# A chunk's plain pair second, rows set aside in SBUF, and another order at the end of the first pass, in a fused FFT and feed-forward kernel

## The chip, the core and the metric

One core of a Trainium2 chip runs the kernel. The metric is the time of one execution on the device, in microseconds (us); several executions are timed and the median is given.

## The reference

The input `x` is 4 batches of 3008 rows of 256 numbers. The first stage is a Fourier filter, the second a feed-forward network over all 12,032 rows:

```python
X = np.fft.rfft(x, axis=1)
Yr = Xr @ w_r - Xi @ w_i + b_r          # 256 x 256 weights
Yi = Xr @ w_i + Xi @ w_r + b_i
Y  = soft_threshold(Yr, 0.01) + 1j * soft_threshold(Yi, 0.01)
y  = np.fft.irfft(Y, n=3008, axis=1)    # becomes 12032 rows of 256
h  = y @ w_in                            # 256 -> 2048
g  = np.maximum(h, 0) + alpha * np.minimum(h, 0)
out = g @ w_out                          # 2048 -> 256
```

## The kernel before

Every float32 operand of a large product is held as a high and a low part, and a product is three matmuls (high x high, low weight x high, high x low). PSUM is eight banks: four of pool `ps_f`, two of `ps_h`, two of `ps_o`.

**The Fourier stage** is a chain of small matmul groups a, b, m, c (L375 to L578) for each batch, all of which take banks of `ps_f`. Its last link turns 376 rows at a time (a group `dg`) back to the row domain: `s_dmm` (L612) makes two banks `ps_d`, and `s_dpart` (L616) splits them into the high and low tiles (`yh`, `yl`) of a chunk of 512 rows; ACT writes the high part (L629) and DVE subtracts for the low part (L631). Since 376 does not divide 512, many groups have rows for two chunks. The tiles of a chunk are opened by `y_open`; there are two sets, so the third chunk in a row must wait for the last use of the first.

**The feed-forward network, first form.** Nine chunks (`CC`) are worked on while the Fourier stage of batches 1 to 3 runs between their steps. A step (`l1_step`, L664) makes one of the 16 tiles of 128 hidden columns: six matmuls into `ps_h` (L659), ACT makes q (L669), DVE q (L670), ACT the high part (L672), and DVE or POOL the low part (L674). `l2_step` does the products of the step two before with `w_out` (L683 to L685 in `products`). Chunks 0 and 1 are interleaved (the first pass), because the second half of the weights is still being made from the raw weights (`conv_second`: L283, L277 to L280, L286, L287), pumped a piece at a time from inside the steps; `PAT` says how many pieces each step pumps. When a chunk is through, `turn` (L697) transposes its two accumulators on DVE (L701) into `oT`, of which there is one buffer, and `put` issues the stores of `oT` on the SP queue (L329) behind everything queued there.

**The second form.** The last 15 chunks (numbers n = 0 to 14; the last has 256 rows) go in pairs t = 0 to 7 of hidden tiles, by a Strassen-like scheme: `s_l1` (L745) makes two tiles (L659; ACT L751, DVE L752), `s_sums` (L756) makes seven operands (ACT L767, L778, L779; DVE L773, L775, L776, L777, L780; POOL L781), and `s_l2` (L828) does seven half-width products into four accumulators p and q (`ps_o`) and u and v (`ps_f`). One pair of each chunk, that in `PLAIN`, is done without the scheme: `z_parts` (L784) makes the high parts on ACT (L788) and the two low parts on POOL and DVE (L789), and `s_l2` does four full-width products into p and q. In the kernel before, `PLAIN` is pair 0. At the end of a chunk `s_out` (L849) folds the four accumulators: two copies on ACT (L855, L856) and six operations on DVE (L857 to L862).

The order is written out by hand. In step k of the second form the program emits: the first-layer tiles of pair k, the products of pair k - 2, at a chunk's end `s_out`, then `s_sums` of pair k. Every engine works through its instructions in this order. So at step (n + 1, t = 1) DVE has L752 twice, then `s_out` of chunk n, then the sums of pair 1; only then comes L752 of pair 2, which frees the `ps_h` bank that the first-layer matmuls of pair 3 write.

Of the kernel before, what the change touches and what calls it, by code (L numbers as in the profile page):

```python
# [9 lines left out]
F32 = mybir.dt.float32  # L10
# [5 lines left out]
AF = mybir.ActivationFunctionType  # L16
# [80 lines left out]
def fft_mix_moe(ctx, tc, x, w_r, w_i, b_r, b_i, w_in, w_out, alpha, la, rb, lc, rd, lf, cf, sel, out):  # L97
# [3 lines left out]
    CT = C // 128  # L101
    FT = DFF // 128
    R = 32
    CH = 4
# [13 lines left out]
    work = ctx.enter_context(tc.tile_pool(name="work", bufs=2))  # L118
    dram = ctx.enter_context(tc.tile_pool(name="dram", bufs=4, space=bass.MemoryType.DRAM))
    ps_f = ctx.enter_context(tc.tile_pool(name="ps_f", bufs=4, space=bass.MemoryType.PSUM))  # L120
    ps_h = ctx.enter_context(tc.tile_pool(name="ps_h", bufs=2, space=bass.MemoryType.PSUM))
    ps_o = ctx.enter_context(tc.tile_pool(name="ps_o", bufs=2, space=bass.MemoryType.PSUM))

    V, G, A, PE = nc.vector, nc.gpsimd, nc.scalar, nc.tensor

    def f(t):
        return t.bitcast(F32)
# [27 lines left out]
    FH = FT // 2  # L155
# [424 lines left out]
    zt, yt = {}, {}  # L580
# [8 lines left out]
    def d_mm(t, ct):  # L589
        ps = ps_f.tile([128, CH, 128], F32, tag="f", name="ps_d")  # L590
        for i in range(CH):
            PE.matmul(ps[:, i, 0:NP], t[:, i, 128 * ct:128 * ct + 128], rd_s, start=True, stop=True)  # L592
        return ps
# [9 lines left out]
    def d_parts(dg):  # L603

        s, e = TOK * dg, TOK * dg + TOK
        for c in range(s // SC, (e - 1) // SC + 1):
            a, z = max(s, SC * c), min(e, SC * (c + 1))
            yield c, (a - s) // CH, (z - s) // CH, a - SC * c, z - SC * c

    ds = {}  # L610

    def s_dmm(dg):  # L612
        t = zt.pop((dg // NCH, dg % NCH))
        ds[dg] = [d_mm(t, ct) for ct in range(CT)]

    def s_dpart(dg, c):  # L616
        parts = []
        for k, n0, n1, a, z in d_parts(dg):
            if k == c:
                for ct in range(CT):  # L620
                    ps = ds[dg][ct][:, :, n0:n1]
                    ys = [y[ct] for y in yt[c]]
                    if c == LASTC:
                        hi, lo = (y[:, a:z].rearrange("p (n i) -> p n i", i=CH) for y in ys)
                        parts.append((ps.rearrange("p i n -> p n i"), hi, lo))
                    else:
                        parts.extend(s_dput(ps, ys, a // CH, z // CH))
        for src, hi, lo in parts:
            A.activation(out=hi, in_=src, func=AF.Copy)  # L629
        for src, hi, lo in parts:  # L630
            V.tensor_tensor(out=lo, in0=src, in1=f(hi), op=ALU.subtract)  # L631

    def s_dput(ps, ys, u, u1):

        ys = [y.rearrange("p (g i j) -> p g i j", i=CH, j=32) for y in ys]
        n = 0
        while u < u1:
            if u % 32 == 0 and u1 - u >= 32:
                w = (u1 - u) // 32 * 32
                src = ps[:, :, n:n + w].rearrange("p i (g j) -> p g i j", j=32)  # L640
                dst = [y[:, u // 32:(u + w) // 32] for y in ys]
            else:
                w = min(u1, u // 32 * 32 + 32) - u
                src = ps[:, :, n:n + w]
                dst = [y[:, u // 32, :, u % 32:u % 32 + w] for y in ys]
            yield src, *dst
            u += w
            n += w
# [28 lines left out]
    def block(m, h):  # L677
        w = wo_h[m // FH][:, m % FH].rearrange("p w (c h) -> p w h c", h=2)
        return w[:, 0, h], w[:, 1, h]

    def products(prods):
        for (wh, wl), (gh, gl), o, first, last in prods:
            PE.matmul(o, wh, gh, start=first, stop=False)  # L683
            PE.matmul(o, wl, gh, start=False, stop=False)  # L684
            PE.matmul(o, wh, gl, start=False, stop=last)  # L685
# [18 lines left out]
    HS = SC // 2  # L704
    PR = FT // 2
# [37 lines left out]
    sg, sa, sq = {}, {}, {}  # L743
# [12 lines left out]
    def s_sums(n, t):  # L756
        q = sq.pop((n, t))
        if n == NS2 - 1 or t in PLAIN:
            z_parts(n, t, q)
# [24 lines left out]
    def z_parts(n, t, q):  # L784
        g = []
        for j, tags in enumerate((("xh", "Yh"), ("xl", "Yl"))):
            hi, lo = (work.tile([128, SC], F32R, tag=tag, name="zg")[:, 0:q.shape[2]] for tag in tags)
            A.activation(out=hi, in_=q[:, j], func=AF.Copy)  # L788
            (V if j else G).tensor_tensor(out=lo, in0=q[:, j], in1=f(hi), op=ALU.subtract)  # L789
            g.append((hi, lo))  # L790
        sg[n, t] = g
# [35 lines left out]

    def s_l2(n, t):  # L828
        if t == 0:
            sa[n] = [ps_o.tile([128, 2, HS], F32, tag="o", name="ps_o") for _ in range(2)]  # L830
        if t == 1:
            sa[n] += [ps_f.tile([128, 2, HS], F32, tag="f", name="ps_o") for _ in range(2)]
        if t in PLAIN:
            for j, g in enumerate(sg.pop((n, t))):
                products([(block(2 * t + j, h), g, sa[n][h].rearrange("p k n -> p (k n)"), (t, j) == (0, 0), False)
                     for h in range(2)])
            return
        r, z = t == 1, t == PR - 1
        b11, b22, b21, t1, t3, t2, t4 = sg.pop((n, t))
        s1, s2, s3, s4 = ([x[:, t] for x in sw[k]] for k in range(4))  # L840
        p, q, u, v = sa[n]
        products([(block(2 * t, 0), b11, u[:, 0], r, False), (block(2 * t + 1, 0), b21, p[:, 1], False, False),
             (s4, b22, p[:, 0], False, z), (s3, t3, v[:, 0], r, False),
             (s1, t1, v[:, 1], False, z), (s2, t2, u[:, 1], False, z),
             (block(2 * t + 1, 1), t4, q[:, 1], False, z)])

    so = {}

# [36 lines left out]
    J = 2  # L885
# [5 lines left out]
    MP = [2.5, 3.5, 3.5, 3.5, 3.5, 4, 4, 4.5]  # L891
    MM, M2, CM = 1.5, 3, 6
    SLAG = 2
    PLAIN = (0,)
    PAT = [0, 0] + [1, 1, 2] * 10
    NG = R // 2
    EARLY = 4
# [14 lines left out]
    with tc.manual_schedule():  # L912
# [98 lines left out]
        for dg in range(2):  # L1011
            s_dmm(dg)
            s_dpart(dg, 0)
# [4 lines left out]
        put()  # L1018

        steps = [(c, m) for c in range(J) for m in range(FH)]  # L1020
        steps += [(c, m + j) for m in range(FH, FT, 2) for c in range(J) for j in range(2)]
        steps += [(c, m) for c in range(J, CC) for m in range(FT)]
        NS = len(steps)
        todo = {}
# [1 line left out]
        def at(i, fn, *args, when=todo):  # L1026
            when.setdefault(i, []).append((fn, args))

        at(0.5, y_open, 1)
        at(0.5, s_dpart, 1, 1)  # L1030
        at(4.5, s_dmm, 2)
        at(4.5, s_dpart, 2, 1)
        at(5.5, y_open, 2)
        at(5.5, s_dpart, 2, 2)
        at(29, load_lc)
# [6 lines left out]
        for dg in range(3, B * NCH):  # L1042
            cs = [c for c, *_ in d_parts(dg)]
            i = FT * (cs[-1] - 1)
            if cs[-1] > CC:
                break
            if len(cs) == 2:
                i -= 2.5
                at(i, s_dmm, dg)
                at(i, s_dpart, dg, cs[0])  # L1050
                at(FT * (cs[-1] - 1) - 1, s_dpart, dg, cs[1])
            else:
                i += 8
                at(i, s_dmm, dg)
                at(i, s_dpart, dg, cs[0])
            at(i - 4, d_load, dg // NCH, dg % NCH)
        for b in range(B - 1):
            if b == 0:
                for g in range(FILL, NG):
                    i = 4 * (g - FILL) + 8  # L1060
# [4 lines left out]
            else:  # L1065
                for g in range(NG):
                    i = AO[b + 1] + (5 * g // 2) / 2
# [5 lines left out]
            for q in range(NPAIR):  # L1073
                i = BO[b + 1] + BP * q
# [15 lines left out]
        i = NS - 17  # L1090
# [10 lines left out]
        for dg in range(dg, B * NCH):  # L1101
            cs = [c for c, *_ in d_parts(dg)]
# [36 lines left out]
        for k in range(len(spairs) + SLAG):  # L1139
            do(pre, k)  # L1140
            if k < len(spairs):
                s_l1(*spairs[k])
            do(post, k)
            put()
            if k < SLAG:
                l2(NS - 1 + k)
            if k >= SLAG:
                n, t = spairs[k - SLAG]
                if n == NS2 - 1:
                    z_l2(t)  # L1150
                else:
                    s_l2(n, t)
                    if t == PR - 1:
                        s_out(n)
            if k < len(spairs):
                s_sums(*spairs[k])
            if k >= SLAG and t == 1 and n:
                s_turn(n - 1)
# [33 lines left out]
```

## Time and profile before

| | |
|---|---|
| median of 3 runs | 1401.27 us (1400.9 to 1404.81) |
| profiled execution, its own time | 1404.03 us |
| its span, first to last instruction | 1402.3 us |
| PE (TensorE matmuls) busy | 1351.0 us, 96% of the span |
| DVE, ACT, POOL busy | 1042.4, 729.2, 376.3 us |
| mean granted TensorE clock | 0.988 of full speed |

A busy share is a mean over stages with different limits. The first form with the Fourier stage runs from about 102 to 704 us of the span, the second form from there to the end. A granted clock of 1.00 is 2.4 GHz and one of 0.50 is 1.2 GHz.

### The profile page before, as it was taken

How to read it: one execution, taken by the hardware profiler on the slowest of the kernel's cores; microseconds unless marked ns; L12 is line 12 of the kernel's file. 1: busy time of each engine (PE TensorE's matmuls, PEld its weight loads, DVE VectorE, ACT ScalarE, POOL GpSimd, SP SyncE). 2: the span in 40 equal slices, each digit the busy share in tenths (PEclk: the TensorE clock that was granted, in tenths of full speed). 3: DMA queues.
4: the chain of work that ended last, by engine and by line, in shares of the span. 5: the costliest groups of instructions: out<-in, count | busy, mean ns of one | idle time of the engine just before them, and what ended most of it. 6: DMA issues, size and time to landing. Idle time of an engine off the chain costs nothing.

```text
span 1402.3 us, 22147 instructions
## 1 busy us (share of the span) xinstructions
PE 1351.0 (96%) x7866; PEld 1173.4 (84%) x7866; DVE 1042.4 (74%) x1843; ACT 729.2 (52%) x1423; POOL 376.3 (27%) x366
## 2 busy tenths in 40 slices
PE   9999998899999999999999999999999999999998
PEld 5978777788888888888888988898888889888988
DVE  2767866667777767677777787788778877877786
ACT  3556544545455544444555555565555555555554
POOL 3843552212222222222222221221212222222222
PEclk9999999999999999999999999999999999999999
DMA  8973333332243312120110110011011001101000
GB/s 224 250 219 97 104 102 101 103 107 84 65 131 94 104 62 87 38 83 24 27 38 12 27 38 7 21 28 27 12 27 28 15 24 27 27 12 28 16 16 24
DMA packets 103759, 89.74 MB, mean 64 GB/s; under 512 B 62446, under 2 KB 85849, under 8 KB 103648
## 3 DMA queue, kind: packets, MB, share of 16 engines
q1 hardware_dynamic: 95744, 77.68, 19.7%
q0 software_dynamic: 4912, 7.76, 2.0%
q10 hardware_dynamic: 2992, 2.88, 0.6%
q8 instruction: 62, 1.02, 0.3%
q14 instruction: 49, 0.40, 0.1%
HBM read 50.76 MB, written 34.34 MB: 61 GB/s over the span
## 4 chain that ended last, share of the span: by engine, by line
PE 66%; DVE 9%; ACT 2%; issue 2%; DMA 0%; POOL 0%; DVEq 0%; SPq 0%; ACTq 0%
PE ps_h L659 29%; PE ps_o L683 8%; PE ps_o L684 8%; PE ps_o L685 8%; PE ps_m L493 4%; PE ps_d L592 3%; PE ps_b L430 2%; DVE sq L752 1%; DVE dl L776 1%; DVE q L670 1%; DVE c L859 1%; DVE t L773 1%; DVE c L862 1%; ACT sq L751 1%; DVE Yt L537 1%
## 5 line engine op out<-in xcount | busy, mean ns | idle before, releaser
L659 PE MATMUL ps_h<-yh,w 128*128 128x512 f32 (+1 forms) x1472 | 502.3, 396 | 26.3 <-DVE sq L752 26.3
L659 PEld LDWEIGHTS ps_h<-yh,w 128*128 128x128 f32 x1472 | 280.3, 192 | 87.8 <-DVE sq L752 32.7
L659 PE MATMUL ps_h<-yl,w 128*128 128x512 f32 (+1 forms) x736 | 289.7, 394 | 0.0
L781 POOL TENSOR_TENSOR l<-t,h 128x512 fp32r<-128x512 f32 x98 | 126.8, 1294 | 503.7 <-ACT h L779 483.6
L752 DVE SCALAR_TENSOR_TENSOR sq<-sq,beta_s,ps_h 128x512 f32<-128x512 f32 (+1 forms) x240 | 168.1, 725 | 72.6 <-ACT sq L751 72.1
L672 ACT ACTIVATE gh<-q 128x512 fp32r<-128x512 f32 x144 | 90.9, 632 | 160.4 <-DVE q L670 160.3
L674 POOL TENSOR_TENSOR gl<-q,gh 128x512 fp32r<-128x512 f32 x69 | 91.7, 1329 | 281.0 <-ACT gh L672 266.5
L670 DVE SCALAR_TENSOR_TENSOR q<-q,beta_s,ps_h 128x512 f32<-128x512 f32 x144 | 106.9, 743 | 73.7 <-ACT q L669 72.9
L659 PEld LDWEIGHTS ps_h<-yl,w 128*128 128x128 f32 x736 | 141.0, 192 | 22.9 <-DVE yl L631 0.2
L751 ACT ACTIVATE sq<-ps_h 128x512 f32<-128x512 f32 (+1 forms) x240 | 132.7, 578 | 46.7 <-PE ps_h L659 44.8
L767 ACT ACTIVATE dh<-sq 128x768 fp32r<-128x768 f32 x98 | 83.0, 847 | 79.9 <-DVE sq L752 63.2
L683 PE MATMUL ps_o<-gh,w 128*128 128x512 f32 x288 | 116.4, 404 | 2.1 <-DVE oT L701 2.1
L779 ACT ACTIVATE h<-t 128x512 fp32r<-128x512 f32 x98 | 62.0, 633 | 104.8 <-DVE t L777 81.5
L685 PE MATMUL ps_o<-gl,w 128*128 128x512 f32 x288 | 114.4, 397 | 0.9 <-POOL gl L674 0.8
L684 PE MATMUL ps_o<-gh,w 128*128 128x512 f32 x288 | 114.3, 397 | 0.0
L669 ACT ACTIVATE q<-ps_h 128x512 f32<-128x512 f32 x144 | 85.2, 592 | 55.1 <-PE ps_h L659 53.0
L776 DVE TENSOR_TENSOR dl<-sq,dh 128x768 fp32r<-128x768 f32 x98 | 93.3, 952 | 0.0
L674 DVE TENSOR_TENSOR gl<-q,gh 128x512 fp32r<-128x512 f32 x75 | 59.3, 791 | 45.1 <-ACT gh L672 45.1
L778 ACT ACTIVATE h<-t 128x512 fp32r<-128x512 f32 x98 | 61.8, 630 | 44.7 <-DVE t L773 44.1
L685 PE MATMUL ps_o<-l,sw_a 128*128 128x256 f32 x294 | 82.0, 279 | 0.0
L683 PE MATMUL ps_o<-h,sw_a 128*128 128x256 f32 x294 | 81.9, 279 | 0.0
L773 DVE TENSOR_TENSOR t<-sq 128x512 f32<-128x512 f32 x98 | 67.5, 689 | 2.4
(184 smaller groups left out, 3002.4 us busy)
## 6 DMA issues: line engine op xcount, KB each, us to landing
zt<-zd SPq DMA_DIRECT2D x32, 384.0 KB
zd<-zst SPq DMA_DIRECT2D x37, 256.0 KB
ad<-ast SPq DMA_DIRECT2D x48, 192.0 KB
bt<-ad SPq DMA_DIRECT2D x72, 128.0 KB
out<-oT SPq DMA_DIRECT2D x248, 32.0 KB
xt<-in_x SPq DMA_DIRECT2D x21, 320.0 KB
cw_s<-in_moe_w_in SPq DMA_DIRECT2D x8, 512.0 KB
cw_s<-in_moe_w_out SPq DMA_DIRECT2D x8, 512.0 KB
```

The lines of the kernel that those rows point to most:

```text
L659: PE.matmul(ps, wi_h[m // FH][:, w, ct, 128 * (m % FH):128 * (m % FH) + 128], a[ct][:, 0:n], start=(k == 0), stop=(k == 3 * CT - 1))
L669: A.activation(out=q, in_=ps, func=AF.Relu, scale=-1.0)
L670: V.scalar_tensor_tensor(out=q, in0=q, scalar=beta_s[:, m:m + 1], in1=ps, op0=ALU.mult, op1=ALU.add)
L672: A.activation(out=hi, in_=q, func=AF.Copy)
L674: (V if by_v else G).tensor_tensor(out=lo, in0=q, in1=f(hi), op=ALU.subtract)
L683: PE.matmul(o, wh, gh, start=first, stop=False)
L684: PE.matmul(o, wl, gh, start=False, stop=False)
L685: PE.matmul(o, wh, gl, start=False, stop=last)
L751: A.activation(out=q[:, j], in_=ps, func=AF.Relu, scale=-1.0)
L752: V.scalar_tensor_tensor(out=q[:, j], in0=q[:, j], scalar=beta_s[:, m:m + 1], in1=ps, op0=ALU.mult, op1=ALU.add)
L776: V.tensor_tensor(out=dl, in0=q[:, HS:], in1=f(dh), op=ALU.subtract)
L781: G.tensor_tensor(out=l24, in0=t24, in1=f(h24), op=ALU.subtract)
```

## The change

Three edits, and one thing that goes with them.

1. `PLAIN` becomes pair 1. Pair 0 of a chunk now goes through the scheme and is the one that starts the four accumulators, so all four are opened at t = 0. In the plain pair, now second, the first matmul into q is cut into two of 256 columns, because one half of q holds sums by then and the other does not.
2. `s_daside` copies the rows of a group that belong to the later chunk from PSUM to a tile in SBUF (tag `zt`), on ACT, two copies for a group; `s_dpart` of the later chunk then reads that tile. It is called for groups 2, 4, 5, 6, 8, 9, 10 and 12, in the first form alone, right behind the earlier chunk's `s_dpart`.
3. The first pass ended with tiles 8 to 15 in turns, two of chunk 0 and two of chunk 1. Now tiles 8 to 11 go so, and then come tiles 12 to 15 of chunk 0 and tiles 12 to 15 of chunk 1. So in steps 26 and 27 stand tiles 14 and 15 of chunk 0, which were in steps 28 and 29; tiles 12 and 13 of chunk 1 go the other way.

```diff
+    def s_daside(dg, c):
+        n0, n1 = next((n0, n1) for k, n0, n1, *_ in d_parts(dg) if k == c)
+        t = work.tile([128, CT, CH, 86], F32, tag="zt", name="hd")
+        for ct, ps in enumerate(ds[dg]):
+            A.activation(out=t[:, ct, :, 0:n1 - n0], in_=ps[:, :, n0:n1], func=AF.Copy)
+        ds[dg] = [t[:, ct] for ct in range(CT)]
+        moved[dg] = n0
...
     def s_l2(n, t):
         if t == 0:
-            sa[n] = [ps_o.tile([128, 2, HS], F32, tag="o", name="ps_o") for _ in range(2)]
-        if t == 1:
-            sa[n] += [ps_f.tile([128, 2, HS], F32, tag="f", name="ps_o") for _ in range(2)]
+            sa[n] = [ps_o.tile([128, 2, HS], F32, tag="o", name="ps_o") for _ in range(2)] \
+                + [ps_f.tile([128, 2, HS], F32, tag="f", name="ps_o") for _ in range(2)]
...
+                        if (j, h) == (0, 1) and w is wh and g is gh:
+                            for k in range(2):
+                                PE.matmul(o[:, HS * k:HS * k + HS], w, g[:, HS * k:HS * k + HS], start=False, stop=False)
+                        else:
+                            PE.matmul(o, w, g, start=False, stop=False)
...
-        r, z = t == 1, t == PR - 1
+        r, z = t == 0, t == PR - 1
...
-    PLAIN = (0,)
+    PLAIN = (1,)
...
-        steps += [(c, m + j) for m in range(FH, FT, 2) for c in range(J) for j in range(2)]
+        steps += [(c, m + j) for m in range(FH, FT - 4, 2) for c in range(J) for j in range(2)]
+        steps += [(c, m) for c in range(J) for m in range(FT - 4, FT)]
...
+        at(4.5, s_daside, 2, 2)
...
                 at(i, s_dpart, dg, cs[0])
+                at(i, s_daside, dg, cs[1])
                 at(FT * (cs[-1] - 1) - 1, s_dpart, dg, cs[1])
```

## Rows read from the trace of the kernel before

**Rows 1.** The page: busy time, share of the span and instructions of each engine.

```profile
PE 1351.0 (96%) x7866; PEld 1173.4 (84%) x7866; DVE 1042.4 (74%) x1843; ACT 729.2 (52%) x1423; POOL 376.3 (27%) x366
```

**Rows 2.** Waits of PE, whole run: us in total, times, longest us.

```profile
PE ps_h L659 <- DVE sq L752: 26.3, 15, 1.9
PE ps_m L493 <- DVE Xl L455: 5.7, 1, 5.7
```

**Rows 3.** Chain that ended last, in order of time: start, us, what.

```profile
765.17 3.02 PE ps_h L659 x12
...
861.28 4.61 PE ps_h L659 x12
868.37 2.75 PE ps_h L659 x12
...
1341.94 3.01 PE ps_h L659 x12
```

**Rows 4.** Windows: us, PE busy, granted clock (PEclk), DMA share, GB/s.

```profile
863.00:864.00 1.00, 1.00 (x3) 0.50 0.00 0
```

**Rows 5.** Timeline of one chunk's end: start, us, engine, instruction [idle before <-releaser].

```profile
903.03 0.39 ACT L855 ACTIVATE se<-ps_o 128x256 f32<-128x256 f32 x1 [1.51 <-PE ps_o L685]
...
903.44 0.42 DVE L857 TENSOR_TENSOR su<-ps_o,se 128x256 f32<-128x256 f32 x1 [1.15 <-ACT se L855]
...
905.94 0.39 PE L683 MATMUL ps_o<-zg,w 128*128 128x512 f32 x1
...
906.02 0.69 DVE L862 TENSOR_TENSOR c<-ps_o,se 128x512 f32<-128x512 f32 x1
...
906.63 0.68 DVE L773 TENSOR_TENSOR t<-sq 128x512 f32<-128x512 f32 x1
...
906.76 0.19 PEld L683 LDWEIGHTS ps_o<-zg,w 128*128 128x128 f32 x1 [0.40 <-DVE c L862]
...
908.89 0.69 DVE L780 TENSOR_TENSOR l<-t,h 128x512 fp32r<-128x512 f32 x1
...
910.24 1.41 DVE L752 SCALAR_TENSOR_TENSOR sq<-sq,beta_s,ps_h 128x512 f32<-128x512 f32 x2 [0.66 <-ACT sq L751]
...
911.04 0.50 PE L659 MATMUL ps_h<-yh,w 128*128 128x512 f32 x1 [1.91 <-DVE sq L752]
```

**Rows 6.** Groups by line, 700 to 1340 us: busy, mean ns of one, idle before.

```profile
L789 DVE TENSOR_TENSOR zg<-sq,zg 128x512 fp32r<-128x512 f32 x14 | 15.7, 1123 | 17.9 <-ACT zg L788 17.9
...
L789 POOL TENSOR_TENSOR zg<-sq,zg 128x512 fp32r<-128x512 f32 x14 | 18.1, 1296 | 21.5 <-PE ps_o L684 15.2 <-ACT zg L788 6.3
```

**Rows 7.** Timeline of DVE, the two steps behind that end.

```profile
915.28 1.40 DVE L752 SCALAR_TENSOR_TENSOR sq<-sq,beta_s,ps_h 128x512 f32<-128x512 f32 x2 [0.64 <-ACT sq L751]
...
920.81 1.37 DVE L752 SCALAR_TENSOR_TENSOR sq<-sq,beta_s,ps_h 128x512 f32<-128x512 f32 x2
```

**Rows 8.** Timeline of DVE and of SP's queue, chunks 0 and 1 turned.

```profile
199.86 1.31 DVE L701 STREAM_TRANSPOSE oT<-ps_o 128x512 f32<-128x512 f32 x2
...
212.28 1.31 DVE L701 STREAM_TRANSPOSE oT<-ps_o 128x512 f32<-128x512 f32 x2 [6.18 <-DMA bt<-ad]
...
201.20 9.78 SPq L329 DMA_DIRECT2D out<-oT  x20
```

**Rows 9.** Timeline of PE (step 26) and POOL, end of the first pass.

```profile
178.91 0.39 PE L659 MATMUL ps_h<-xh,w 128*128 128x512 f32 x1
...
179.91 1.34 POOL L287 TENSOR_TENSOR w<-conv 128x512 fp32r<-128x512 f32 x1 [1.58 <-DVE conv L286]
...
186.60 1.30 POOL L287 TENSOR_TENSOR w<-conv 128x512 fp32r<-128x512 f32 x1
```

**Rows 10.** Timeline of PE, three stops at banks of `ps_f`.

```profile
271.92 0.71 PE L385 MATMUL ps_a<-xh,la_s 94*96 94x512 f32 x1 [2.11 <-DVE Yc L531]
...
280.47 0.48 PE L385 MATMUL ps_a<-xh,la_s 94*96 94x512 f32 x1 [1.97 <-ACT zst L572]
...
589.01 0.71 PE L493 MATMUL ps_m<-wr_s,Xh 128*128 128x256 f32 x4 [1.31 <-DVE Yc L531]
```

More of the change, by code (lines that the diff above doesn't have):

```diff
@@ L614, in s_dmm @@
         ds[dg] = [d_mm(t, ct) for ct in range(CT)]
+    def s_daside(dg, c):
[5 more added lines that the diff above has]
+        moved[dg] = n0
+    moved = {}
     def s_dpart(dg, c):
@@ L619, in s_dpart @@
             if k == c:
+                n0, n1 = n0 - moved.get(dg, 0), n1 - moved.get(dg, 0)
                 for ct in range(CT):
@@ L829, in s_l2 @@
         if t == 0:
-            sa[n] = [ps_o.tile([128, 2, HS], F32, tag="o", name="ps_o") for _ in range(2)]
-        if t == 1:
-            sa[n] += [ps_f.tile([128, 2, HS], F32, tag="f", name="ps_o") for _ in range(2)]
+            sa[n] = [ps_o.tile([128, 2, HS], F32, tag="o", name="ps_o") for _ in range(2)] \
+                + [ps_f.tile([128, 2, HS], F32, tag="f", name="ps_o") for _ in range(2)]
         if t in PLAIN:
-            for j, g in enumerate(sg.pop((n, t))):
-                products([(block(2 * t + j, h), g, sa[n][h].rearrange("p k n -> p (k n)"), (t, j) == (0, 0), False)
-                     for h in range(2)])
+            for j, (gh, gl) in enumerate(sg.pop((n, t))):
+                for h in range(2):
+                    (wh, wl), o = block(2 * t + j, h), sa[n][h].rearrange("p k n -> p (k n)")
+                    for w, g in ((wh, gh), (wl, gh), (wh, gl)):
+                        if (j, h) == (0, 1) and w is wh and g is gh:
[3 more added lines that the diff above has]
+                            PE.matmul(o, w, g, start=False, stop=False)
             return
-        r, z = t == 1, t == PR - 1
+        r, z = t == 0, t == PR - 1
         b11, b22, b21, t1, t3, t2, t4 = sg.pop((n, t))
@@ L841, in s_l2 @@
         p, q, u, v = sa[n]
-        products([(block(2 * t, 0), b11, u[:, 0], r, False), (block(2 * t + 1, 0), b21, p[:, 1], False, False),
+        products([(block(2 * t, 0), b11, u[:, 0], r, False), (block(2 * t + 1, 0), b21, p[:, 1], r, False),
              (s4, b22, p[:, 0], False, z), (s3, t3, v[:, 0], r, False),
              (s1, t1, v[:, 1], False, z), (s2, t2, u[:, 1], False, z),
-             (block(2 * t + 1, 1), t4, q[:, 1], False, z)])
+             (block(2 * t + 1, 1), t4, q[:, 1], r, z)])
     so = {}
```

## The prediction

> **What bounds the kernel now.** The page's busy table comes first: PE is busy for 96% of the span, the next engine for 74% [rows 1]. So time can be won only where PE stands still or runs slowly, and the second view is the list of what PE waits for. Its longest entry by far is the first-layer matmul (L659) waiting for DVE's L752, 15 times and up to 1.9 us each; behind it come single waits of the first form, the longest 5.7 us [rows 2].
>
> The third view, the chain that ended last, tells where those 15 are. Through the second form it is PE work, broken once in a chunk: thirteen groups of twelve first-layer matmuls, the first at 765.17 and the last at 1341.94, take 3.01 to 4.61 us where the other groups take 2.75 [rows 3]. Each is the restart after a stop. Six took 3.0 us; seven took 4.5 to 4.6, and in one of those the windows show a granted clock of 0.50, so 1.2 GHz [rows 4]. The stop before a 4.6 and before a 3.0 is the same 1.91 us, so whether the clock falls is not decided by this stop's length alone.
>
> The fourth view, the timeline of one chunk's end, shows the reason for the stop [rows 5]. DVE folds the old chunk (L857 at 903.44 to the end of L862 at 906.71), then makes the sums of pair 1 (L773 at 906.63 to the end of L780 at 909.58), and only then does L752 (910.24), for whose first half PE waits until 911.04. PE had begun the plain pair's products at 905.94. Twelve matmuls at 0.23 (2.75 / 12) last 2.78, so PE could have gone on at 908.72. The stop thus costs 2.32 us, a short wait for L862 inside the plain pair included.
>
> **Part 1, the plain pair second.** In the step with the fold, DVE now has only the plain pair's single low part in place of five sums. I follow the new order through [rows 5]. The fold ends at 906.71 as before. The low part is a subtraction of 128x512 from two SBUF tiles, as L780 is: 0.69, so it ends at 907.40. ACT's two high parts for it stand behind L856 and are long done. L752's first half then runs from 907.40 to 908.10 (1.41 for two). PE begins the products of pair 0, now seven half-width ones, at 905.94, and they last 2.48 (868.37 - 861.28 - 4.61) [rows 3], so PE wants the bank at 908.42. It is free 0.3 us earlier. The accumulators are free in time: the first product goes into u, read last by L857; p follows 0.35 later, after L859, which ends before 905.5; q comes last, at about 908, after L862.
>
> Does DVE keep up afterwards? With the sums on it, L752 comes 5.04 after the last L752, and 5.53 after it where the two transposes lie between [rows 5, 7]; a step of PE is 2.75 + 2.48 = 5.23. From 907.40 this gives 912.44 and 917.97, against latest times (0.75 ahead of PE's need) of 907.67, 912.90 and 918.13. The smallest slack is 0.16 us; then 0.2 comes back in each step. I take a remaining loss of 0.1 for each chunk, between nothing and 0.5.
>
> So each of the 13 ends gives back 2.32 for the stop and 0.26 for the restart (3.01 - 2.75): 13 x 2.58 = 33.5. The seven slow restarts give 7 x (4.60 - 3.01) = 11.1 more. Less 13 x 0.1, that is **43.3 us**. The end of the last full chunk gains nothing, as the last chunk goes by `z_parts` in any order. The cut matmul is one more of 256 columns in place of half of one of 512, nothing on PE; its weight load lies beside the matmuls. The plain pair's work and that of pair 0 only change places.
>
> Here a page of the Trainium skill speaks against the change. In the trace the plain pair's DVE part lasted 1.12 us, with POOL's part (1.30) running beside it [rows 6], though the same shape took 0.69 alone [rows 5]. The Trainium skill's page "SBUF — State Buffer", section "Who interferes with whom", states that a VectorE instruction with two SBUF inputs contends with a GpSimd instruction that reads SBUF, and by it 0.43 us would be lost whenever the two overlap. In the new order POOL's part starts on ACT's first high part, at about 904.3, and has ended by 905.6, before DVE comes to its own at 906.7; I therefore count 0.69, and the other case is a rival.
>
> **Part 2, the first pass.** Chunk 1's transposes at 212.28 waited 6.18 us, and PE behind them 5.7 [rows 2, 8]. The entry names another DMA, but `oT` has one buffer: chunk 0's transposes end at 201.17, its twenty stores hold SP from 201.20 to 210.98, and 1.3 later DVE goes on. Chunk 0 now ends two steps earlier (a step here is twelve matmuls, 2.76; group 4's matmuls lie between too, so I estimate 7 us for 2 x 2.76 and them) while chunk 1 ends where it did. Without the wait its transposes would have begun at 206.10, and the buffer would be free at 212.28 - 7 = 205.3. The stop goes: 5.7, and 1.6 for the clock after it, as at the slow restarts [rows 3], 7.3 in all.
>
> The same edit asks for weights earlier. Tile 14 of chunk 0 moves to step 26, which PE began at 178.91; its third matmul, at 179.37, needs the low part that POOL's L287 finishes at 181.25 [rows 9]: a stop of 1.9. Its second-layer weights are done by L287 at 187.90, and PE wants them in step 28 at about 186.1 (178.91 + 2 x 2.76 + 1.38 + 0.23). The first stop pushes PE by 1.9, but also the pieces behind tile 14's own ACT and DVE work, and the low part of g of step 26 falls to POOL now (1.30 [rows 6]) between them. I take 1.4 for the second stop, between nothing and 2.7. After such stops the clock may fall (1.6 each, or not): 1.4 for both. Together 4.7, between 1.9 and 7.8. SP's stores of chunk 1 still stand ahead of the Fourier stage's next loads: 0.8 back. Part 2 gives **1.8 us**, from -3 to +5.
>
> **Part 3, rows set aside.** Group 5's two banks are held from step 46 to 47, and there, at 271.92 and 280.47, PE stops at `ps_a` for 2.1 and 2.0 us; while group 9's are held, it stops at `ps_m` for 1.3, at 589.01 [rows 10]. Each time the releaser named is what empties another bank of the same pool. With the banks free after two copies, the second and the third go; of the first, 0.5 (from nothing to 0.9), since the bank must still be copied out. The clock stood low after both of the first two: I count 1.6 for the second and 0.6 for the first. Sum 0.5 + 2.0 + 1.6 + 0.6 + 1.3 = 6.0, from 3.3 to 8.2. The cost is 16 copies on ACT of 40 (group 10) to 344 (group 4) elements; 256 elements took 0.39 [rows 5], so about 5 us of an engine that is half idle [rows 1]. It delays what stands behind it on ACT by 0.1 to 1.0, evacuations that PE needs a step later. I take 0.5, between nothing and 3. Where the cover fails it would be seen as new waits of PE for ACT. The `zt` buffer taken is free: the next load comes ten steps later. **5.5 us.**
>
> **The sum.** 43.3 + 1.8 + 5.5 = 50.6, from the profiled execution's own 1404.0: 1353.4, told as **1354**. This execution is 2.8 above the median of the runs (1401.27), which I put down to how many restarts met a low clock; without stops that difference should vanish, so I subtract from the profiled one.
>
> **The rivals.** *POOL in DVE's way.* The low part takes 1.12 after all, or L861, another two-input subtraction, is held: L752 comes 0.43 later, past the slack of 0.27. Then PE stops for 0.3 and restarts with 0.26 at each of 13 ends (7.3 in place of 1.3), and the clock falls after seven of them or none: 1360 to 1371. For it speaks the 1.12; against it the order of times above.
>
> *The first pass dearer and the asides cheaper than they look*: part 2 at -3, part 3 at 3.3 - 3: 1364.
>
> *The change doesn't do what it says.* DVE's work in a chunk is the same, and if the stop just moves to the next step, the 43.3 are gone and the 7.3 stay: about 1397, not to be told from no change. Against it: DVE gains on PE in each step after the end.
>
> *Slower.* Pair 0's sums (2.95) now stand in front of the fold; should they push the fold, L752 comes later than before. To end above 1405.5, each of the 13 ends must cost 4.0 us more than I count ((1405.5 - 1353.4) / 13). But DVE had 1.15 idle before L857 [rows 5], and the sums add 1.83 to the part that they replace (2.95 - 1.12): the push is 0.7, some 9 us over all ends. It decides only where DVE falls 4 us behind: 1407.
>
> **How the numbers follow.** Chances: the forecast 0.62 (its own range 1346 to 1361), POOL in the way 0.15, the dearer first pass 0.13, the stop that moves 0.06, slower 0.04. The range 1346 to 1371 takes in the first three. 0.3% (4.2 us) is about what a measurement can tell here: faster 0.90, same 0.06, slower 0.04.
>
> **What the new profile would show.** If part 1 is right, PE's waits for L752 shrink from 15 to two or three of the last chunk, the granted clock is 1.00 through the second form, and twelve-matmul groups of 3.0 or 4.6 are gone from the chain. If part 2 is right, L701 has no wait for a DMA near 210, and PE has two stops near 180 and 188 on POOL's L287. If part 3 is right, the two `ps_a` waits become one of some 1.5. The prediction is wrong if L659 still waits for L752 at every chunk's end, or if DVE's backlog shows as a wait at the step after the transposes.

## The result, and the profile after

The changed kernel takes 1361.72 us (median of 4 runs, 1361.24 to 1362.94), beside 1403.04 for the kernel before in the same comparison: a ratio of 0.9705, interval 0.9682 to 0.9728, so 41.4 us faster (0.0295 x 1403). The prediction was 1354.0 with a range of 1346 to 1371: the direction held, and with it the mechanism of part 1, which gave nearly all of the gain; that of part 2 did not. The time came out 7.7 us above the forecast, just above the likeliest case's own range (1346 to 1361). The profiled execution took 1362.94, with a span of 1361.1.

The page of the changed kernel, as in [rows 1]; the last line is the granted clock in 40 slices:

```profile
PE 1332.3 (98%) x7880; PEld 1165.9 (86%) x7880; DVE 1032.6 (76%) x1843; ACT 731.2 (54%) x1439; POOL 375.2 (28%) x366
PEclk9999998999999999999999999999999999999999
```

PE does 14 matmuls more (one in each full chunk) and is busy for 18.7 us less; the mean granted clock rose from 0.988 to 0.996 of full speed. Lines of the new file stand 12 later than those of the old from `s_daside` on, and 17 later in `s_out`: L671 is the first-layer matmul (before L659), L764 is DVE's step ahead of the sums (L752), L801 the plain pair's low part (L789), L713 the transposes (L701). What PE waits for, as in [rows 2]:

```profile
PE ps_h L671 <- DVE q L682: 5.9, 1, 5.9
...
PE ps_h L671 <- POOL w L287: 1.7, 1, 1.7
PE ps_o L696 <- POOL w L287: 1.7, 1, 1.7
PE ps_h L671 <- DVE sq L764: 1.5, 2, 1.3
PE ps_a L385 <- ACT hd L621: 1.5, 1, 1.5
```

The 15 waits for L752 (26.3 us) have become two, of 1.5 us together: one of 1.25 inside the last chunk, one of 0.26 in the first chunk of the second form, at 715.77. But the list has a new first line: a single wait of 5.9 for L682 where one of 5.7 stood for L455.

The end of the same chunk as in [rows 5]:

```profile
895.48 0.42 DVE L874 TENSOR_TENSOR su<-ps_o,se 128x256 f32<-128x256 f32 x1 [0.48 <-ACT se L872]
...
896.32 1.30 POOL L801 TENSOR_TENSOR zg<-sq,zg 128x512 fp32r<-128x512 f32 x1 [1.87 <-ACT zg L800]
...
898.05 0.69 DVE L879 TENSOR_TENSOR c<-ps_o,se 128x512 f32<-128x512 f32 x1
...
898.66 0.68 DVE L801 TENSOR_TENSOR zg<-sq,zg 128x512 fp32r<-128x512 f32 x1
...
899.26 1.40 DVE L764 SCALAR_TENSOR_TENSOR sq<-sq,beta_s,ps_h 128x512 f32<-128x512 f32 x2
...
900.45 0.40 PE L671 MATMUL ps_h<-yh,w 128*128 128x512 f32 x1
...
909.85 1.36 DVE L764 SCALAR_TENSOR_TENSOR sq<-sq,beta_s,ps_h 128x512 f32<-128x512 f32 x2
...
911.20 0.40 PE L671 MATMUL ps_h<-yh,w 128*128 128x512 f32 x1
```

Behind the fold DVE has one subtraction of 0.68 in place of the sums, and L764's first half ends at 899.96 (899.26 + 1.40 / 2). PE wants that bank at 900.45 and takes it without a wait: 0.49 to spare. The window around this end (us, PE busy, granted clock, DMA share, GB/s) is at full clock, as are all of 50 us from 700 to 1350:

```profile
850.00:900.00 50.00, 50.00 (x317) 1.00 0.08 20
```

**Where the 41 us came from** is read by lining up the same steps in the two profiles. Near the end of the first form, in the third step from its last, ACT's q starts at 698.83 (before 696.67), so the changed kernel is 2.2 us *behind* there. The last chunk's one long wait ends at 1339.73 (before 1380.84). The stretch between the two, nearly all of the second form, takes 640.90 in place of 684.17: 43.27 us less, against a forecast of 43.3. In these two profiles the whole miss lies ahead of 699.

There the timeline has this. DVE, SP's queue and PE at the end of the first pass, as in [rows 8 and 9]:

```profile
181.93 0.74 PE L671 MATMUL ps_h<-yh,w 128*128 128x512 f32 x2 [1.74 <-POOL w L287]
...
190.62 0.51 PE L696 MATMUL ps_o<-gh,w 128*128 128x512 f32 x1 [1.71 <-POOL w L287]
...
196.19 1.31 DVE L713 STREAM_TRANSPOSE oT<-ps_o 128x512 f32<-128x512 f32 x2
...
197.52 8.66 SPq L329 DMA_DIRECT2D out<-oT  x20
...
207.48 0.69 DVE L229 TENSOR_TENSOR wd_f<-wm_f 128x512 f32<-128x512 f32 x1 [8.29 <-DMA bt<-ad]
...
210.08 0.75 DVE L682 SCALAR_TENSOR_TENSOR q<-q,beta_s,ps_h 128x512 f32<-128x512 f32 x1 [1.18 <-ACT q L681]
...
210.88 0.79 PE L671 MATMUL ps_h<-yh,w 128*128 128x512 f32 x1 [5.92 <-DVE q L682]
```

The transposes no longer wait, as forecast. But L229 (`combine_mix`, which makes the difference of two filter weights) now waits 8.29 us on DVE, and PE behind it 5.92. The windows behind that stop (us, PE busy, granted clock, DMA share, GB/s) show half the clock, 1.2 GHz:

```profile
210.00:215.00 5.00, 4.12 (x10) 0.50 0.06 20
215.00:216.00 1.00, 1.00 (x4) 0.50 0.00 0
```

The wait's named releaser is the same `bt<-ad` as in [rows 8], and it is as little the cause here: SP is through with issuing the twenty stores of `oT` at 206.18 (197.52 + 8.66), and DVE goes on 1.30 later, as it did before (212.28 - 210.98). When the stores themselves have landed, these rows do not show. The code says why L229 should care for `oT`'s stores:

```python
d = work.tile([128, CT, C], F32, tag="os", name="wd_f", bufs=1)   # L228, combine_mix
```

`oT` is a tile of the same tag "os" with one buffer. In the old order of steps `combine_mix` ran ahead of chunk 0's turn (the transposes at 199.86 [rows 8]), as DVE's timeline of before shows:

```profile
194.08 1.82 DVE L229 TENSOR_TENSOR wd_f<-wm_f 128x512 f32<-128x512 f32 x1
```

With chunk 0's turn two steps earlier it runs behind it, and the buffer is not free.

Of the rows set aside, PE's stops at banks of `ps_f`, as in [rows 10]:

```profile
276.99 0.48 PE L385 MATMUL ps_a<-xh,la_s 94*96 94x512 f32 x1 [1.49 <-ACT hd L621]
...
319.41 0.39 PE L561 MATMUL ps_c<-Yh,lc_s 128*128 128x256 f32 x1 [1.28 <-ACT ast L399]
```

The first of the three stops went from 2.11 to 1.49, the second and third are gone; a stop of 1.28 at 319.41 is new.

### The profile page after: what moved, and what is told of

It reads as the page before. It is cut to its first block, busy times and chain, and to the rows that moved or that the text cites. A ratio compares the mean times of both kernels' runs of the same rounds, so it can differ in the third digit from the quotient of the medians.

```text
span 1361.1 us, 22169 instructions
## 1 busy us (share of the span) xinstructions
PE 1332.3 (98%) x7880; PEld 1165.9 (86%) x7880; DVE 1032.6 (76%) x1843; ACT 731.2 (54%) x1439; POOL 375.2 (28%) x366
## 3 DMA queue, kind: packets, MB, share of 16 engines
q10 hardware_dynamic: 2992, 2.88, 0.7%
## 4 chain that ended last, share of the span: by engine, by line
PE 84%; DVE 6%; ACT 3%; issue 3%; DMA 2%; SPq 1%; POOL 1%; ACTq 0%; DVEq 0%; POOLq 0%
PE ps_h L671 34%; PE ps_o L696 10%; PE ps_o L697 10%; PE ps_o L695 10%; PE ps_m L493 5%; PE ps_d L592 4%; PE ps_o L853 3%; PE ps_b L430 2%; PE ps_a L382 2%; DVE q L682 1%; PE ps_m L480 1%; SPq L329 1%; ACT gh L684 1%; DVE gl L686 1%; ACT q L681 1%
## 5 line engine op out<-in xcount | busy, mean ns | idle before, releaser
L671 PE MATMUL ps_h<-yh,w 128*128 128x512 f32 (+1 forms) x1472 | 494.5, 391 | 9.3 <-DVE q L682 5.9
L671 PEld LDWEIGHTS ps_h<-yh,w 128*128 128x128 f32 x1472 | 276.1, 189 | 64.2 <-DVE q L682 6.9
L671 PE MATMUL ps_h<-yl,w 128*128 128x512 f32 (+1 forms) x736 | 285.6, 388 | 0.0
L764 DVE SCALAR_TENSOR_TENSOR sq<-sq,beta_s,ps_h 128x512 f32<-128x512 f32 (+1 forms) x240 | 166.3, 723 | 59.7 <-ACT sq L763 59.1
L686 POOL TENSOR_TENSOR gl<-q,gh 128x512 fp32r<-128x512 f32 x69 | 91.5, 1326 | 283.7 <-ACT gh L684 260.3
L682 DVE SCALAR_TENSOR_TENSOR q<-q,beta_s,ps_h 128x512 f32<-128x512 f32 x144 | 106.9, 742 | 71.8 <-ACT q L681 71.0
L671 PEld LDWEIGHTS ps_h<-yl,w 128*128 128x128 f32 x736 | 139.5, 189 | 22.7 <-DVE yl L643 0.2
L791 ACT ACTIVATE h<-t 128x512 fp32r<-128x512 f32 x98 | 62.0, 633 | 104.2 <-DVE t L789 102.1
L686 DVE TENSOR_TENSOR gl<-q,gh 128x512 fp32r<-128x512 f32 x75 | 58.0, 774 | 45.4 <-ACT gh L684 42.7
L697 PEld LDWEIGHTS ps_o<-gl,w 128*128 128x128 f32 x288 | 56.3, 195 | 13.5 <-POOL gl L686 1.6
```

The costliest lines, as they stand in the source:

```text
L671: PE.matmul(ps, wi_h[m // FH][:, w, ct, 128 * (m % FH):128 * (m % FH) + 128], a[ct][:, 0:n], start=(k == 0), stop=(k == 3 * CT - 1))
L682: V.scalar_tensor_tensor(out=q, in0=q, scalar=beta_s[:, m:m + 1], in1=ps, op0=ALU.mult, op1=ALU.add)
L686: (V if by_v else G).tensor_tensor(out=lo, in0=q, in1=f(hi), op=ALU.subtract)
L764: V.scalar_tensor_tensor(out=q[:, j], in0=q[:, j], scalar=beta_s[:, m:m + 1], in1=ps, op0=ALU.mult, op1=ALU.add)
```

## The experiments

Each kernel is compared with the kernel before on the same chip: 1401.39 (median of 16) for e1 to e4, 1402.7 (median of 14) for e5 to e8.

**The three edits, each alone on the kernel before.** The theory was that part 2 gave its own gain back at L229; the rival, that part 1 gave less than 43 and the first pass was only dear at L287.

*e1*, the plain pair second and nothing else:

```diff
-    PLAIN = (0,)
+    PLAIN = (1,)
```

(with the new `s_l2` of the change).

> The kernel before with the plain pair second and nothing else of the change. Theory of the prediction: the 13 stops of PE for DVE's L752 and the low clock after seven of them go, 43 us less than the kernel before (about 1360 on a kernel before of 1403), and the granted clock is 1.00 through the second form. Rival: the gain of the whole change comes partly from the two other edits, which then would have to make up more than 5 us; plain alone gives under 36.

Measured: 1360.7, ratio 0.9706 (0.9693 to 0.9718), 41.2 us faster. PE's waits for L752 shrink to two, 0.27 in the first chunk and 1.25 in the last, and the clock is 1.00 in all windows of 50 us from 750 to 1350. The three stops at `ps_f` (2.1, 2.0 and 1.3) and the one for L455 are still there:

```profile
PE ps_m L493 <- DVE Xl L455: 5.3, 1, 5.3
...
PE ps_h L659 <- DVE sq L752: 1.5, 2, 1.3
```

Part 1 alone gives what the whole change gives.

*e2*, the order of the first pass and nothing else:

```diff
-        steps += [(c, m + j) for m in range(FH, FT, 2) for c in range(J) for j in range(2)]
+        steps += [(c, m + j) for m in range(FH, FT - 4, 2) for c in range(J) for j in range(2)]
+        steps += [(c, m) for c in range(J) for m in range(FT - 4, FT)]
```

> The kernel before with the other order at the end of the first pass and nothing else. Theory now: the weights' difference buffer (wd_f) and oT share one buffer (tag os); chunk 0's transposes now come ahead of wd_f, so DVE waits for the stores at L229 in place of L701, PE's stop of 5.7 is still there at another place, and the two stops on POOL's L287 (1.7 each) are new: 3 to 6 us slower than the kernel before. Rival, the step as predicted: the stop of 5.7 is gone and the edit gives 1.8 (from 3 slower to 5 faster); what the whole change lacks to the forecast was lost elsewhere.

Measured: 1404.42, ratio 1.0029 (1.0011 to 1.0047): 4.1 us slower (1.5 to 6.6). PE's waits in e2 (its lines are those of before):

```profile
PE ps_h L659 <- DVE sq L752: 26.3, 15, 1.9
PE ps_h L659 <- DVE q L670: 5.9, 1, 5.9
...
PE ps_h L659 <- POOL w L287: 1.7, 1, 1.7
```

The stop for L455 is gone and that for L670 has its length. The edit alone loses time, though by little more than the noise: the 13 stops for L752 are still in this kernel, and its 11 runs have mean clocks of 0.984 to 0.990.

*e3*, `s_daside` and its two calls, and nothing else:

```diff
+        at(4.5, s_daside, 2, 2)
...
+                at(i, s_daside, dg, cs[1])
```

> The kernel before with the rows set aside in SBUF and nothing else. Theory: the second stop at ps_a (2.0) and that at group 9's banks (1.3) go, and the low clock after the second, 4 to 6 us faster than the kernel before. Rival: the 16 copies on ACT delay evacuations by as much as the banks give, within 2 us of the kernel before.

Measured: 1397.6, ratio 0.997 (0.9958 to 0.9982): 4.2 us faster (2.5 to 5.9). The stops that were to go are gone, and behind the first, now 1.50, the clock is at 1.00, where it stood at 0.50 from 272 to 275 before. The stop at L561 that the changed kernel has at 319.41 is here too:

```profile
313.47 0.39 PE L561 MATMUL ps_c<-Yh,lc_s 128*128 128x256 f32 x1 [0.63 <-ACT ast L399]
```

The three changes sum to -41.2 + 4.1 - 4.2 = -41.3, where the whole gives -41.4: they do not act on each other within what can be told.

**The cause of the new stop.** *e4* is the changed kernel with another buffer for `wd_f`:

```diff
-        d = work.tile([128, CT, C], F32, tag="os", name="wd_f", bufs=1)
+        d = work.tile([128, CT, C], F32, tag="zst", name="wd_f", bufs=3)
```

> The changed kernel with wd_f in a buffer of another tag (zst, three buffers, idle there). Theory: DVE's wait of 8.3 at L229 was for oT's stores alone; it goes, and with it PE's stop of 5.9 and the low clock after it: 6 to 8 us faster than the changed kernel, so 49 to 51 us faster than the kernel before. Rival: the wait is for the DMA that the trace names (bt<-ad), or it moves on to chunk 1's transposes, which need oT four steps later; then under 2 us faster than the changed kernel.

Measured: 1352.68, ratio 0.9651 (0.9639 to 0.9664), by the ratios 7.6 us below the changed kernel. DVE in e4:

```profile
196.81 1.31 DVE L713 STREAM_TRANSPOSE oT<-ps_o 128x512 f32<-128x512 f32 x2
...
199.74 1.60 DVE L229 TENSOR_TENSOR wd_f<-wm_f 128x512 f32<-128x512 f32 x1
...
210.28 1.31 DVE L713 STREAM_TRANSPOSE oT<-ps_o 128x512 f32<-128x512 f32 x2
```

L229 and both turns go without a wait, and PE has no stop between 200 and 216, at full clock. That the shared buffer was the cause is shown: nothing else was changed. The same piece of PE's work lies between these two rows, first of the changed kernel, then of e4:

```profile
204.56 0.40 PE L697 MATMUL ps_o<-gl,w 128*128 128x512 f32 x1
...
217.06 0.48 PE L671 MATMUL ps_h<-yh,w 128*128 128x512 f32 x1
```

```profile
205.18 0.40 PE L697 MATMUL ps_o<-gl,w 128*128 128x512 f32 x1
...
208.99 0.47 PE L671 MATMUL ps_h<-yh,w 128*128 128x512 f32 x1
```

It takes 12.50 us there and 3.81 here. Of the 8.7 between, 5.9 are the stop and most of the rest is half clock, which lasts until past 216. The 7.6 by the ratios agrees with it within the intervals.

*e5* is e4 with the second half of the weights pumped one step earlier, for the two stops at L287:

```diff
-    PAT = [0, 0] + [1, 1, 2] * 10
+    PAT = [0] + [1, 1, 2] * 10 + [1]
```

> The kernel with wd_f in its own buffer, and the pieces of the weights pumped one step earlier (PAT begins with one 0 in place of two). Theory: PE's two stops on POOL's L287 (1.7 each) are there because the pieces come one step too late; one step is 2.8 us, so both go: 3 us less than with wd_f in its own buffer alone. Rival: the pieces hang on the raw weights' loads or on DVE and POOL, which are as late as before; within 1 us.

Measured: 1348.36, ratio 0.9614 (0.9598 to 0.963), the fastest kernel of this study: 54 us under the kernel before and, by the ratios, 12.8 under the changed one. The first stop at L287 is gone, the second is 0.7. By the ratios it is 5.2 under e4, where 3 was expected; the stops give 2.8, the intervals allow 3, and where the rest comes from is not shown.

*e8* is the changed kernel with the old order of steps.

> The changed kernel with the old order at the end of the first pass. Theory: the edits add up, so it is 3 to 6 us faster than the changed kernel, with PE's stop of 5.7 for chunk 1's transposes back and the two stops on POOL's L287 gone. Rival: the asides change what the order edit costs; within 1 us of the changed kernel.

Measured: 1355.94, ratio 0.9666 (0.9652 to 0.9681), 5.5 us under the changed kernel. It has the old stop for L455 (4.9) and none for L287. So on the changed kernel too the order edit costs time. With `wd_f` in its own buffer (e4) it no longer does: e4 is 2.1 us below e8, but their intervals overlap, so a gain from the order is not shown.

**Why the second place for the plain pair.** *e6* makes the plain pair the third (`PLAIN = (2,)`), so that the pair with the sums lies in the step with the fold again.

> The changed kernel with the plain pair third in place of second (PLAIN is pair 2); the work is the same. Theory: what counts is that the pair with the light DVE work falls into the step of the fold; third, the five sums stand behind the fold again, PE stops 13 times for DVE's L752 (now L764), 1.5 to 2.2 us each with the restart, and the clock falls after some: 26 to 45 us slower than the changed kernel. Rival: the gain comes from opening all four accumulators with pair 0, whose first product needs only u; then within 5 us of the changed kernel.

Measured: 1408.9 (9 runs, 1405.27 to 1420.65), ratio 1.0069 (1.0041 to 1.0097): 51 us above the changed kernel by the ratios (47 by the medians), slower even than before. DVE and PE in e6:

```profile
912.66 0.69 DVE L879 TENSOR_TENSOR c<-ps_o,se 128x512 f32<-128x512 f32 x1
913.27 0.68 DVE L785 TENSOR_TENSOR t<-sq 128x512 f32<-128x512 f32 x1
...
915.60 0.69 DVE L792 TENSOR_TENSOR l<-t,h 128x512 fp32r<-128x512 f32 x1
916.95 1.41 DVE L764 SCALAR_TENSOR_TENSOR sq<-sq,beta_s,ps_h 128x512 f32<-128x512 f32 x2 [0.66 <-ACT sq L763]
917.75 0.50 PE L671 MATMUL ps_h<-yh,w 128*128 128x512 f32 x1 [2.54 <-DVE sq L764]
```

It is [rows 5] again: fold, sums, L764, and PE behind them, at all 13 ends. The loss is more than the 26 to 45 us that were expected: the stops are longer than before's 1.91 (twelve of 2.53 or 2.54, one of 2.88), and 11 of the 13 meet a low clock in the profile, where it was 7 before. DVE is not later for it: from the start of the fold to PE's restart it is 7.66 us (910.09 to 917.75) beside 7.60 before (903.44 to 911.04). PE is earlier, since between the two it has pair 0's half-width products (2.48 by the prediction's rows) and not the plain pair's (2.78 and the wait for L862). All four accumulators are opened with pair 0 here too, so the rival is out: what the change won hangs on which pair lies beside the fold.

**How much room part 1 has.** *e7* puts the other low part of the plain pair on DVE too, one more subtraction behind the fold:

```diff
-            (V if j else G).tensor_tensor(out=lo, in0=q[:, j], in1=f(hi), op=ALU.subtract)
+            (V if j or n < NS2 - 1 else G).tensor_tensor(out=lo, in0=q[:, j], in1=f(hi), op=ALU.subtract)
```

> The changed kernel with both low parts of the plain pair on DVE (in the full chunks), POOL's part being one more subtraction of 0.68 on DVE in the step of the fold. The trace shows PE's need 0.49 us after the first half of L752 (now L764) is done. Theory: the slack is used up and PE stops 0.2 us at each of 13 ends, restarts included 0.2 to 0.5 each: 3 to 7 us slower than the changed kernel, up to 18 where the clock falls too. Rival: DVE has more room than that, or POOL's part was itself what DVE waited for; within 2 us.

Measured: 1367.12, ratio 0.9741 (0.9725 to 0.9756), 5 us above the changed kernel. DVE and PE at a chunk's end, and the chain's piece that begins there:

```profile
849.80 1.28 DVE L801 TENSOR_TENSOR zg<-sq,zg 128x512 fp32r<-128x512 f32 x2
851.01 1.40 DVE L764 SCALAR_TENSOR_TENSOR sq<-sq,beta_s,ps_h 128x512 f32<-128x512 f32 x2
...
851.80 0.50 PE L671 MATMUL ps_h<-yh,w 128*128 128x512 f32 x1
```

```profile
851.80 3.02 PE ps_h L671 x12
```

Thirteen groups of 3.02 to 3.06 are back in the chain, none of 4.6. 0.6 us of DVE work more uses up the 0.49 (1.28 in place of 0.68), so the room is no larger than that. No run adds less, so that all of the 0.49 could be used is not shown.

## Why the prediction was right, and where it failed

**Part 1: right.** By the profiles it gave 43.27 against 43.3, by e1's ratio 41.2 (39.5 to 43.0). The forecast was worked out from the one profiled execution of before, with its seven slow restarts, and that stands 2.8 above the median of its runs; this would account for the difference, which no run shows by itself. L764's waits at the chunk ends and the restarts of 3.0 and 4.6 are gone; one restart of 3.06 is left, at 715.77, and the clock is 1.00 in all windows of 50 us. The order of times was right in its turns: the fold, one subtraction of 0.69 (measured 0.68), L764, a bank free 0.3 ahead of its use (measured 0.49). At the step with the transposes 0.16 was forecast and 0.67 was left: L764's first half was done at 910.53 (909.85 + 0.68), and PE took the bank at 911.20. DVE went as forecast (L764 10.59 later, forecast 5.04 + 5.53 = 10.57), but PE's two steps took 10.75 (911.20 - 900.45), since the plain pair's products, 2.78 and not 2.48, lie in the first of them; I had taken 2 x 5.23. (Twelve times 0.23 is 2.76; the 2.78 of the prediction is what the trace shows, and the 0.02 change nothing.)

**POOL in DVE's way: the rival did not come about, but its mechanism is there.** POOL's part ran from 896.32 to 897.62 and DVE's began at 898.66, so the order of times that spoke against it held, and L801 took 0.68. In e6 the two overlap:

```profile
918.50 1.29 POOL L801 TENSOR_TENSOR zg<-sq,zg 128x512 fp32r<-128x512 f32 x1 [0.73 <-ACT zg L800]
...
919.14 1.20 DVE L801 TENSOR_TENSOR zg<-sq,zg 128x512 fp32r<-128x512 f32 x1 [0.78 <-ACT zg L800]
```

DVE's takes 1.19 to 1.21 in all 13 of these chunks (a mean of 1.12 in [rows 6]); L229, a subtraction of the same shape, took 0.69 at 207.48 with POOL idle, and 1.60 in e4, where POOL's L686 ran from 199.50 to 200.79. The Trainium skill's page "SBUF — State Buffer", section "Who interferes with whom", states that a VectorE instruction with two SBUF inputs contends with a GpSimd instruction that reads SBUF; the traces agree, 0.68 alone and 1.20 beside it.

**Part 2: the step "The stop goes" failed.** It counted 7.3 back for the stop of 5.7 and its clock. The wait of the transposes did go, but `oT`'s buffer has a second user, `wd_f`, which the new order puts behind chunk 0's stores; the stop went from the transposes to L229 and kept its length (5.92) and a half clock behind it. So part 2 gave -4.1 (e2, -6.6 to -1.5) in place of +1.8, below the stated -3 to +5, though by less than the noise (the terms shown for it add up to -1.3 to 4.6). Of the 50.6 forecast the ratio gives 41.4; of the 9.2 that are missing, 5.9 are part 2, 1.3 part 3, and 2.1 what e1 gave less than 43.3, each to within the intervals given. With `wd_f` elsewhere (e4) the stop does go. What the order is then worth is 3.5 by -4.1 + 7.6 and 2.1 by e4 against e8; both are near the forecast 1.8, and neither is clear of noise. That e4's 1352.68 is so close to 1354 is in part luck: its kernel before takes 1401.39 and not the 1404.0 that was subtracted from, and parts 1 and 3 gave 3.4 less than forecast. Of the other terms of part 2, the two stops at L287, forecast 1.9 and 1.4, were 1.74 and 1.71. The 1.4 for the clock behind them was not lost: the granted clock stayed at 1.00 from 181 to 195. Whether the 0.8 for the loads behind chunk 1's stores was lost, the runs do not tell. The reading that the entry's named DMA was not the cause was right, and it should have led to the question who else uses the tag.

**Part 3: right in mechanism, and in size within the noise** (4.2 by e3, 2.5 to 5.9, against 5.5, bounds 0.3 to 8.2 with the cost of the copies). The 8.2 is more than the terms shown reach: 7.4, with 1.6 for both clocks. The first `ps_a` stop fell to 1.49 as forecast, and the low clock behind it, counted at 0.6, went altogether; the second and third stops went. The new stop of 1.28 at 319.41 waits for ACT's L399, as a cost of the copies would. The runs bear that out: all six other kernels with the copies stop there, and none without them (before, e1, e2) does: for 0.63 in e3, e4 and e5, 0.87 in e7, 0.89 in e8 and 1.07 in e6. Why its length differs stays open.

Of the rivals, *the first pass dearer* (1364, part 2 at -3) comes nearest: its sign and its price for part 2 are about right (-3 against -4.1), its place is not, since it put the cost on the stops at L287, and part 3 gave 4.2 and not 0.3. That the time lies in the stated range is thus owed to a range that takes in the rivals: 1361.7 is just outside the forecast's own, and inside the 1360 to 1371 of *POOL in DVE's way*, which did not come about. *The stop moves* and *slower* did not come about either: DVE still had 0.48 idle ahead of the fold (L874 at 895.48), so pair 0's sums did not push it; e6 shows what a stop that moves would have looked like.

## What to carry to other kernels

Where an engine is late once in a chunk, count its work between two uses of the bank that is waited for, and put the lightest unit beside the burst: here that was worth 41 us, and one place further (e6) it was worth less than nothing. Before a step is moved past others, list every tile that shares its buffer's tag, in the order of issue, before and after the move: the stop that the move removes can come back at the next user of the buffer, as it did here. Where the releaser that a wait names has nothing to do with the waiting instruction, look for stores out of its buffer; in both waits here SP had issued the last of them 1.30 us earlier.

## What the runs showed of the hardware that was not expected

That a stop's length alone does not decide the clock behind it, which the prediction read from one profile, holds in three more. With stops of 1.91 us at the 13 chunk ends, 7 restarts of 13 met a low clock in the profile before (twelve matmuls in 4.5 to 4.6 us in place of 3.0), 6 in e2 and 7 in e3. With stops of 2.53 in e6 it was 11 of 13, and with those of 0.05 to 0.42 in e7 none. Two rows of e6's chain, the same work behind the same stop (2.54 and 2.53):

```profile
867.62 4.61 PE ps_h L671 x12
...
1211.27 3.02 PE ps_h L671 x12
```

The time of one kernel varies with it: e6's nine executions are five of 1405.3 to 1408.9 at a mean clock of 0.989 to 0.993 and four of 1415.6 to 1420.7 at 0.981 to 0.983. The 11 us between are about seven restarts of 1.6, an estimate, since only one of them was profiled. In the changed kernel the full chunks have no such stop but one of 0.26, and its four runs lie within 1.7 us.
